# An adaLN transformer block: late K blocks and the Q of chunks 1 to 3 projected between the pairs of the first attention steps

## Chip, cores and metric

One core of one Trainium2 chip runs the kernel. The metric is the device time of one execution in microseconds, the median of the runs. Before the change it is 1879.76 us (three runs, 1879.09 to 1879.83). All times below are microseconds unless marked otherwise.

## What is computed

A transformer block with adaptive layer norm, on x of 2048 rows (S) by 512 (D), 32 heads of 16, and a gated FFN of 1792 columns (F), all in float32:

```python
mod = (silu(c) @ w_mod).reshape(1, 6, 1, 512)
sa, ca, ga, sb, cb, gb = mod[:, 0], ..., mod[:, 5]
h = layernorm(x) * (1 + ca) + sa
q, k, v = split_heads(h @ wqkv)                  # 32 heads, 16 each
p = softmax(q @ k.T * 16 ** -0.5)
x = x + ga * (merge_heads(p @ v) @ wo)
h = layernorm(x) * (1 + cb) + sb
x = x + gb * ((silu(h @ w_gate) * (h @ w_up)) @ w_down)
```

## The kernel before

**Numbers in two parts.** The matmuls run in a rounded format (F32R). To keep accuracy every operand is held as a high part and a low part (the rest), and every product is three matmuls: high x high, high x low, low x high (`mm3`, L205; `accumulate`, L709). "Splitting" a tensor means making these parts: a copy into F32R and a subtraction.

**Projection.** The rows of x go in four chunks of 512. `prep` (L175) normalises a chunk, turns it by transposes and modulates it into `hT[ci]`, high and low. `proj_T(ci, w, m)` (L360) makes one block of 128 columns of Q (w = 0) or K (w = 1) for one chunk: 12 full matmuls into a PSUM bank (four slices of the contraction, three products each), then ACT copies the high part to `prt`, DVE subtracts the low part (L367, L369), and two DMAs on the queue of SyncE (SP) store the three planes to `qd` or `kd` in DRAM (L372, L373). `proj_v` (L388) makes V for 128 rows and leaves it in SBUF as `v_sb`. There are 16 Q blocks, 16 K blocks and 16 V blocks. The class `Stream` (L64) runs a list of such jobs on the PE and, per matmul, lets other generators ("lanes": normalisation `p`, weight splits `w`, modulation vectors `m`) emit one item every so many matmuls.

**Attention.** A unit is one chunk of 512 queries and one group of four heads; 32 units of 16 steps, 512 steps. A step is one block of 128 keys. Its work is four *pairs* and two *P·V halves*. A pair (`pair_of`, L903) is a score matmul (`score`, L500, 50 rows of the array) for the current step and a max matmul (`max_one`, L470, 48 rows) for a step about 20 steps ahead, side by side in the two halves of the array's rows. ACT takes the score's exponential (L508) into one of `PTS` buffers `pt`; DVE reduces the max matmul's bank to row maxima (L481). When a unit's maxima are complete, `max_rows` (L483) turns them and writes them as two more rows of the unit's Q operand, so that the score comes out with its maximum taken off. A P·V half (`pv_step`, L510) is matmuls on four column tiles into bank 7 for half of the queries. Operands are loaded per unit: `load_k` (L462) brings all keys of the head group from `kd` into one of three tiles `kop`, `load_q` (L465) the queries from `qd`.

**PSUM.** Eight banks. Before attention and in plain attention, max matmuls turn through banks 0 to 3 and scores through 4 to 6; bank 7 is P·V's. While FFN work is filled in, it takes banks 3 and 6 (`FBANKS`), max turns through 0 to 2 and scores through 4 and 5.

**Order of the work, written out by hand** (the PE executes in program order, as every engine does):

1. A loop over chunks 0 to 2 (L415) runs the jobs of K, Q and V with the lanes in between.
2. `late` (L836) holds what is left: all of chunk 3, two blocks of chunk 2, and V of chunks 2 and 3: 18 blocks. 48 of their matmuls run at once (L840, L842), the others, 8 or 9 per step, between the max matmuls of 20 lead-in steps (L888 to L897; `LEAD` = 21).
3. The 512 steps. `plain` (L936) does windows of three pairs followed by one or two P·V halves. From step 147 (`STARTS`) each finished chunk's output projection and FFN run half-row matmuls, two side by side on the two halves of the array, between the pairs: `filled` (L949) does eight pairs with places such as `TWO` (0, 3, 2, 2, 2, 2, 1, 0) giving how many of them follow each pair, then P·V.
4. A tail for the last chunk's output projection and FFN.

`close_unit` (L844) does a unit's division by the softmax sum over DRAM and issues the loads for the unit three ahead; `after` (L869) runs what is due at the end of each step. GpSimd (POOL) splits the weights of output projection and FFN once, during the first 128 steps (`split_weights`, L575): it loads raw weights, makes both parts and stores them in `wo_dr`, `gu_dr` and `wd_dr`; the chunks later load both parts. POOL also splits activations during the FFN (L781, L782) and issues half of the operand loads.

Of the kernel before, what the change touches and what calls it, by code (L numbers as in the profile page):

```python
# [43 lines left out]
PTS = 13  # L44
# [4 lines left out]
STARTS = (147, 275, 403)  # L49
TWO = (0, 3, 2, 2, 2, 2, 1, 0)  # L50
# [51 lines left out]
def block_kernel(ctx, tc, x, wqkv, wo, w_gate, w_up, w_down, c, w_mod, out):  # L102
# [33 lines left out]
    gu_dr = dram.tile([NF, P, 4, NK, P], F32, name="gu_dr")  # L136
    wd_dr = dram.tile([NF // FG, P, 2, FG, D], F32, name="wd_dr")
    wo_dr = dram.tile([NK // 2, P, 2, 2, D], F32, name="wo_dr")
# [81 lines left out]

    es_a0 = ExitStack()
# [38 lines left out]
    wqs = [pa0.tile([P, NK, 3 * D], F32R, name=f"wqs{i}") for i in range(2)]  # L260
# [39 lines left out]
    def split_w(src, c0, eng=nc.gpsimd):  # L300
        cols = slice(c0, c0 + P)
        split(wqs[0][:, :, cols], wqs[1][:, :, cols], src, eng)

    def new_hT():
        return [pa0.tile([P, NK, CW], F32R, name=f"hT{i}", tag=f"hT{i}", bufs=2) for i in range(2)]
# [53 lines left out]

    def proj_T(ci, w, m):  # L360
        def job():
            pt = bank("pt")
            col = (0 if w == 0 else D) + m * P

            def post():
                prt = pa0.tile([P, 2, CW], F32R, name="prt", tag="prt", bufs=4)
                nc.scalar.copy(prt[:, 0, :], pt)  # L367
                yield
                nc.vector.tensor_sub(prt[:, 1, :], pt, prt[:, 0, :].bitcast(F32))  # L369
                yield  # L370
                dst = (qd, kd)[w][m * P:(m + 1) * P, :, ci * CW:(ci + 1) * CW]
                nc.sync.dma_start(dst[:, 1 - w:3 - w, :], prt.bitcast(F32))  # L372
                nc.sync.dma_start(dst[:, 2 * w, :], prt[:, 0, :].bitcast(F32))  # L373
            return mm3(pt, lambda a, k: wqs[a][:, k, col:col + P], lambda b, k: hT[ci][b][:, k, :], NK), post()
        return job
# [12 lines left out]
    def proj_v(t):  # L388
        def job():
            pt = bank("pv_")  # L390
            sl = slice((t % 4) * P, (t % 4 + 1) * P)
            h_ = hT[t // 4]

            def post():
                nc.scalar.copy(v_sb[:, t, :, 0:DH], pt.rearrange("p (h d) -> p h d", d=DH))
                yield
            return mm3(pt, lambda a, k: h_[a][:, k, sl], lambda b, k: wqs[b][:, k, 2 * D:3 * D], NK), post()
        return job
# [7 lines left out]
    def load_k0(ci):  # L406
        load_parts(kop[0][:, :, ci * CW:(ci + 1) * CW], kd, 0, ci * CW, (ci + 1) * CW)
# [7 lines left out]
    for ci in range(NC - 1):  # L415
        jobs = [proj_T(ci, w, m) for w, m in kq[:6 if ci == NC - 2 else 8]]
        if ci < NC - 2:
            jobs += [proj_v(4 * ci + t) for t in range(4)]
        hT[ci + 1] = new_hT()
        if ci == 0:  # L420
            jobs[0:2] = [both(*jobs[0:2], 6)]
        if ci == 1:
            sm.add("m", 7, mods(4, 3, lambda e, ev: mod_col(ev, [(modc[:, 2 + e], slice(0, NK), 1.0 - e)])))
        if ci == 2:
            sm.add("m", 6, mods(2, 5, lambda e, ev: mod_row(ev, (ga_bc, gb_bc)[e], (1.0, 0.5)[e])))
        if ci:
            sm.add("p", 5 if ci < NC - 2 else 3, prep(pa, xt[ci + 1], hT[ci + 1], 0, 1))
        for i, _ in enumerate(sm.jobs(jobs)):
            if ci == 0 and i == 5:
                half_prep(1, ev)  # L430
                take(weights_, 2)
                sm.add("w", 5, weights_)
            if ci == 0 and i == 24:
                sm.add("p", 5, prep(pa, xt[1], hT[1], 0, 1))
            if i == 40:
                load_k0(ci)
            if i == 44 and ci + 2 < NC:
                load_x(ci + 2)
        while sm.lanes["p"][1]:
            run(sm.lanes["p"][1].pop(0))  # L440
# [10 lines left out]
    pf = None  # L451
# [10 lines left out]
    def load_k(u):  # L462
        load_parts(kop[u % 3], kd, u % NG, 0, S, nc.gpsimd if u > 2 else nc.sync)

    def load_q(u):  # L465
        ci, g = divmod(u, NG)
        qop[u] = pb.tile([P, 2, CW], F32R, name="qop", tag="qop", bufs=3)
        load_parts(qop[u], qd, g, ci * CW, (ci + 1) * CW, nc.gpsimd if u > 2 else nc.sync)

    def max_one(r):  # L470
# [3 lines left out]
        s, qt, kc = t // 8, t // 2 % 4, t % 2 * 2 + e  # L474
# [35 lines left out]
    def pv_step(i, half):  # L510
# [4 lines left out]
        if kt == 0 and half == 0:  # L515
            pv[u] = single("pv")
            o_[u] = pf.tile([P, CW], F32, name="o", tag="o", bufs=2)
# [10 lines left out]
    def out_a(u, eng):  # L528
        pv.pop(u)
        o = o_.pop(u)  # L530
        dn = pf.tile([P, 16], F32, name="dn", tag="dn", bufs=1)
# [8 lines left out]
    def out_r(u, eng, o):  # L540
        rb = pf.tile([P, CW], F32, name="rb", tag="rb", bufs=1)
# [3 lines left out]
    def out_c(u, eng, mul, o, rb):  # L545
        ci, g = divmod(u, NG)
        on = pf.tile([P, CW], F32, name="on", tag="on", bufs=1)
        mul.tensor_mul(on, o, rb)  # L548
        eng.dma_start(o_dr[ci, g], on)
# [10 lines left out]
    def tile_gu():  # L560
        return pf.tile([P, 4, NK, P], F32R, name="wgu", tag="wgu", bufs=2)

    def tile_wd():
        return pf.tile([P, 2, FG, D], F32R, name="wd", tag="wd", bufs=1)
# [10 lines left out]
    def split_weights():  # L575

        def raw(src, k):
            t = tile_mid().bitcast(F32)
            nc.gpsimd.dma_start(t.rearrange("p e c -> p (e c)").rearrange("p (k c) -> p k c", k=k), src)
            return t  # L580

        def parts(hi, lo, t):
            nc.gpsimd.tensor_copy(hi, t)
            nc.gpsimd.tensor_sub(lo, t, hi.bitcast(F32))

        def store(dst, w):
            nc.gpsimd.dma_start(dst, w.bitcast(F32))

        def cols(m):
            return slice(m * FG * P, (m + 1) * FG * P)  # L590

        srcs = [(wod[:, 2 * k:2 * k + 2, :], 2) for k in range(NK // 2)]
        for m in range(NF // FG):
            srcs += [(wgd[:, :, cols(m)], NK), (wud[:, :, cols(m)], NK), (wdd[:, m * FG:(m + 1) * FG, :], FG)]
        ahead = [raw(*srcs.pop(0)) for _ in range(2)]
        yield

        def following():
            if srcs:
                ahead.append(raw(*srcs.pop(0)))  # L600
            return ahead.pop(0)

        for k in range(NK // 2):
            t = following()
            nc.gpsimd.tensor_mul(t, t, ga_bc[:, None, :].to_broadcast([P, 2, D]))
            w = tile_gu()
            parts(as_wo(w)[:, 0], as_wo(w)[:, 1], t)
            store(wo_dr[k], as_wo(w))
            yield
        for m in range(NF // FG):  # L610
            ws = [tile_gu() for _ in range(FG)]
            for e in range(2):
                t = following()
                src = t.rearrange("p e c -> p (e c)").rearrange("p (k f c) -> p f k c", k=NK, f=FG)
                for f in range(FG):
                    parts(ws[f][:, 2 * e], ws[f][:, 2 * e + 1], src[:, f])
                    if e:
                        store(gu_dr[m * FG + f], ws[f])
# [448 lines left out]
```

## Time and profile before

| | us |
|---|---|
| median of three runs | 1879.76 |
| span of the profiled execution | 1875.6 |
| attention's first score | 189.1 |
| first matmul of the first chunk's output projection (step 147) | 547.9 |
| last max matmul | 1648.8 |

The profile's span is the execution's own time from its first to its last instruction; the runs' times lie some 4 above it. The profile lists for each engine how long it was busy. The engines are PE (TensorE matmuls), PEld (weight loads of the PE, which overlap), DVE (VectorE), ACT (ScalarE), POOL (GpSimd) and SP (SyncE, which here only issues DMAs). A line such as "L481 DVE ... x2048 | 1286.5, 682 | 119.5 <-PE bank L479 72.4" is a group of instructions of one source line: count, busy time in all, mean nanoseconds of one, then the idle time of the engine just before them and what ended most of it. Several matmuls are in flight at once, so the distance between two starts, not the duration of one, tells what a matmul costs.

### The profile page before, as it was taken

The numbers are of one execution on the slowest core, as the hardware profiler recorded it, in microseconds if no ns is written. First come the engines' busy times: TensorE is split into PE (matmuls) and PEld (weight loads), VectorE is DVE, ScalarE is ACT, GpSimd is POOL, SyncE is SP. The second block draws the span as 40 slices with busy tenths as digits, with TensorE's granted clock in tenths as the row PEclk, the third lists the DMA queues.
The fourth block names the chain that finished last, engine by engine and source line by source line (L and its number), as shares of the span: only waits on it lengthen the run. The fifth ranks groups of instructions, "written<-read, shape, count | busy, mean of one in ns | idle before, by whom it ended". The sixth has DMA issues, their size and how long they took to land.

```text
span 1875.6 us, 41002 instructions
## 1 busy us (share of the span) xinstructions
PE 1846.7 (98%) x16996; PEld 1160.4 (62%) x16996; DVE 1541.8 (82%) x2558; ACT 1252.4 (67%) x2406; POOL 415.3 (22%) x498
## 2 busy tenths in 40 slices
PE   7999999999999999999999999999999999999999
PEld 5766444444455766666555667666554566667887
DVE  5548999999999888888999888889999988831643
ACT  4221888888887766777777776677878877674211
POOL 3000454456323211111133111111123011030200
PEclk9999999999999999999999999999999999999999
DMA  8855677766843534554454454453643446243642
GB/s 286 292 198 142 174 183 178 201 167 190 211 86 78 145 102 124 144 124 90 107 124 116 108 127 131 121 122 78 159 86 56 108 92 156 86 159 119 249 180 110
DMA packets 78854, 267.62 MB, mean 143 GB/s; under 512 B 17364, under 2 KB 22484, under 8 KB 57988
## 3 DMA queue, kind: packets, MB, share of 16 engines
q1 hardware_dynamic: 59820, 180.10, 33.0%
q0 software_dynamic: 18160, 84.10, 19.0%
q8 instruction: 133, 2.18, 0.5%
q10 hardware_dynamic: 688, 0.80, 0.1%
q14 instruction: 53, 0.43, 0.1%
HBM read 201.85 MB, written 62.13 MB: 141 GB/s over the span
## 4 chain that ended last, share of the span: by engine, by line
PE 95%; DVE 2%; ACT 2%; DMA 0%; issue 0%; SPq 0%; ACTq 0%; DVEq 0%
PE bank L521 26%; PE bank L506 22%; PE bank L719 19%; PE bank L479 10%; PE bank L729 7%; PE bank L209 7%; DVE mx L481 1%; PE bank L762 1%; PE bank L491 1%; PE bank L162 0%; PE bank L703 0%; DMA wm_ab<-in_w_mod 0%; DVE stt L745 0%; PE bank L279 0%; PE bank L493 0%; PE bank L492 0%
## 5 line engine op out<-in xcount | busy, mean ns | idle before, releaser
L481 DVE TENSOR_REDUCE mx<-bank 128x1 f32<-128x512 f32 x2048 | 1286.5, 682 | 119.5 <-PE bank L479 72.4
L479 PE MATMUL bank<-kop,qop 48*128 48x512 f32 x2048 | 748.0, 432 | 3.6 <-DVE mx L481 3.4
L506 PE MATMUL bank<-qop,kop 50*128 50x512 f32 x2048 | 742.1, 427 | 4.6 <-ACT pt__20499 L508 0.5
L506 PEld LDWEIGHTS bank<-qop,kop 50*128 50x128 f32 x2048 | 347.0, 184 | 305.6 <-issue 63.3
L479 PEld LDWEIGHTS bank<-kop,qop 48*128 48x128 f32 x2048 | 343.9, 184 | 30.7 <-DVE mx L481 14.4
L719 PE MATMUL bank<-act,wgu 64*128 64x512 f32 x1872 | 297.9, 392 | 0.0
L719 PEld LDWEIGHTS bank<-act,wgu 64*128 64x128 f32 x1872 | 188.4, 187 | 30.9 <-DVE m L779 0.3
L548 POOL TENSOR_TENSOR on<-o,rb 128x512 f32<-128x512 f32 x31 | 39.7, 1282 | 442.9 <-DMA rb<-d_dr 304.0
L719 PE MATMUL bank<-wd,mid 64*128 64x512 f32 x912 | 136.5, 397 | 0.0
L781 POOL CAST mid<-m 128x512 fp32r<-128x512 f32 x40 | 24.3, 609 | 430.1 <-PE bank L479 165.5
L719 PEld LDWEIGHTS bank<-wd,mid 64*128 64x128 f32 x912 | 93.3, 185 | 12.0 <-issue 0.8
L209 PE MATMUL bank<-hT,wqs 128*128 128x512 f32 x384 | 95.7, 399 | 2.1 <-DVE prt L369 0.8
L209 PEld LDWEIGHTS bank<-hT,wqs 128*128 128x128 f32 x384 | 70.3, 188 | 24.3 <-issue 6.1
L777 DVE SCALAR_TENSOR_TENSOR q<-th,bank 128x512 f32<-128x512 f32 x56 | 37.7, 673 | 57.4 <-ACT th L773 57.2
L773 ACT ACTIVATE th<-bank 128x512 f32<-128x512 f32 x56 | 33.2, 593 | 58.3 <-PE bank L729 57.9
L793 DVE TENSOR_TENSOR x<-bank,x 128x512 f32<-128x512 f32 x84 | 53.8, 684 | 20.4 <-PE bank L506 20.2
L369 DVE TENSOR_TENSOR prt<-bank,prt 128x512 fp32r<-128x512 f32 x32 | 22.0, 688 | 46.5 <-ACT prt L367 46.5
L367 ACT CAST prt<-bank 128x512 fp32r<-128x512 f32 x32 | 18.8, 587 | 60.2 <-PE bank L209 46.9
L779 DVE TENSOR_TENSOR m<-bank,q 128x512 f32<-128x512 f32 x56 | 38.7, 691 | 21.2 <-PE bank L729 19.1
L729 PE MATMUL bank<-wd,mid 128*128 128x512 f32 x216 | 52.1, 394 | 0.4 <-DVE mid L782 0.3
L782 POOL TENSOR_TENSOR mid<-m,mid 128x512 fp32r<-128x512 f32 x40 | 51.6, 1291 | 3.3
L719 PE MATMUL bank<-wgu,act 64*128 64x512 f32 x288 | 47.7, 394 | 0.1
(6282 smaller groups left out, 5155.0 us busy)
## 6 DMA issues: line engine op xcount, KB each, us to landing
wgu<-gu_dr SPq DMA_DIRECT2D x48, 1024.0 KB
wd<-wd_dr SPq DMA_DIRECT2D x28, 1024.0 KB
kop<-kd SPq DMA_DIRECT2D x33, 768.0 KB
kop<-kd POOLq DMA_DIRECT2D x29, 768.0 KB, 8.5
gu_dr<-wgu POOLq DMA_DIRECT2D x14, 1024.0 KB, 14.1
kd<-prt SPq DMA_DIRECT2D x16, 512.0 KB
qd<-prt SPq DMA_DIRECT2D x16, 512.0 KB
kop<-gu_dr SPq DMA_DIRECT2D x8, 1024.0 KB
```

Of the source, the lines that this page charges most:

```text
L209: nc.tensor.matmul(pt, lhs(a, k), rhs(b, k), start=(n == 0), stop=(n == 3 * nk - 1))
L479: nc.tensor.matmul(pm, qop[u][rows, s, qt * P:(qt + 1) * P], kop[u % 3][rows, s, kc * CW:(kc + 1) * CW], start=True, stop=True)
L481: nc.vector.tensor_reduce(mx[u][:, b, s, qt, kc:kc + 1], pm, op=ALU.max, axis=AX.X)
L506: nc.tensor.matmul(sp, kop[u % 3][rows, h // 2, kt * P:(kt + 1) * P], qop[u][rows, h // 2, :], start=True, stop=True)
L521: nc.tensor.matmul(pv[u][32 * h:32 * h + 32, cols], v_flat[:, e0:e0 + 32], p_[h][:, cols], start=(kt == 0 and half == 0), stop=(kt == 15), ...
L548: mul.tensor_mul(on, o, rb)
L719: nc.tensor.matmul(outs[e], lhs(e, a, k)[rows], rhs(b, k)[rows], start=(ph == 0 and j == 0), stop=(j == z and (ph == 1 or trade is not None)),
L729: nc.tensor.matmul(outs[e], lhs(e, a, k), rhs(b, k), start=(j == 0), stop=(j == z))
L777: nc.vector.scalar_tensor_tensor(q, th, 1.0, outs[0], op0=ALU.add, op1=ALU.mult)
L779: nc.vector.tensor_mul(m32, outs[1], q)
L782: (nc.gpsimd if slow else nc.vector).tensor_sub(mid[:, 1, :], m32, mid[:, 0, :].bitcast(F32))
L793: nc.vector.tensor_add(ch.x2[:, t, :], outs[e], ch.x2[:, t, :])
```

## The change

Projection before attention is cut to chunk 0's Q and K, the first K block (m = 0) of chunks 1 and 2, and V of chunks 0 and 1. `late` becomes the first K block of chunk 3, the second K block of chunks 1 to 3, and V of chunks 2 and 3. The other 18 blocks, K blocks 2 and 3 of chunks 1 to 3 and all of Q of chunks 1 to 3, are made in attention's first 99 steps.

```diff
+HELD = 99
+SOON = (0, 1, 1, 1, 1, 0)
+LATER = (0, 0, 1, 1, 1, 0)
-PTS = 13
+PTS = 14
...
-    for ci in range(NC - 1):
-        jobs = [proj_T(ci, w, m) for w, m in kq[:6 if ci == NC - 2 else 8]]
...
+    first_jobs = [proj_T(0, w, m) for w, m in kq]
+    first_jobs[0:2] = [both(*first_jobs[0:2], 6)]
+    first_jobs += [proj_T(1, 1, 0)] + [proj_v(t) for t in range(4)] + [proj_T(2, 1, 0)] + [proj_v(4 + t) for t in range(4)]
+    for i, _ in enumerate(sm.jobs(first_jobs)):
...
+        if i == 24:
+            hT[1] = new_hT()
+            sm.add("p", 3, prep(pa, xt[1], hT[1], 0, 1))
...
+        if i == 90:
+            hT[2] = new_hT()
+            sm.add("p", 3, prep(pa, xt[2], hT[2], 0, 1))
...
+        if i == 157:
+            hT[3] = new_hT()
+            sm.add("p", 2, prep(pa, xt[3], hT[3], 0, 1))
...
-    late = sm.jobs([proj_T(last, w, m) for w, m in kq[:1] + kq[2:]] + [proj_T(last - 1, w, m) for w, m in kq[6:]] +
-                   [proj_T(last, *kq[1])] + [proj_v(4 * ci + t) for ci in (last - 1, last) for t in range(4)])
+    late = sm.jobs([proj_T(3, 1, 0)] + [proj_T(ci, 1, 1) for ci in range(1, NC)] + [proj_v(t) for t in range(8, NT)])
     ones_rows(1)
     load_q(0)
-    take(late, 22)
-    load_k0(last)
-    take(late, 26)
...
-        take(late, 9 if i % 2 else 8)
+        take(late, 7)
...
+    def late_pair(ci, w, ms):
+        fill = [banks[b] for b in FBANKS]
+        wts = [weight_T(w, m) for m in ms]
+
+        def after():
+            posts_ = [keep_T(ci, w, m, fill[e]) for e, m in enumerate(ms)]
+            for _ in range(3):
+                for p in posts_:
+                    next(p, None)
+        return accumulate(fill, lambda e, a, k: wts[e](a)[:, k, :], lambda b, k: hT[ci][b][:, k, :], NK, after, True)
+
+    def late_pairs():
+        for ci in range(1, NC):
+            yield from late_pair(ci, 1, (2, 3))
+        for ci in range(1, NC):
+            for ms in ((0, 1), (2, 3)):
+                yield from late_pair(ci, 0, ms)
+
+    def mixed(places, work):
+
+        nonlocal four, bank
+        four, bank = three, Turn(4, 5)
+        for k in places:
+            pair_of()
+            take(work, k)
+        pvs(3 if done > 8 else 0, True)
+        end_steps()
...
+    work = late_pairs()
+    while done < 4 * HELD:
+        mixed(SOON if done < 108 else LATER, work)
```

`keep_T` is the tail of the old `proj_T`: the copy, the subtraction and the two stores. In `accumulate` with halves, one `take` emits two matmuls on 64 rows each, one for each of two output blocks; a pair of blocks takes 24 of them. Unit 0's max matmuls are reordered so that all of them for key chunk 0 come first, then chunk 1, and so on, and `load_k0(3)` moves into the fourth lead-in step.

The weights wqkv and all `hT` now have to live until step 99, so memory is found elsewhere: the FFN's tiles (`pf`) are opened only after step 99, the multiplication of a unit's output is done in place, and GpSimd no longer keeps split weights in DRAM. `relay_gu` copies the raw gate and up weights from DRAM to DRAM in the order of use (28 DMAs on POOL's queue, one block every six steps from step 8 on); `relay_weights` scales the output and down weights by their modulation rows from step 102 to 129. The chunks load one raw copy (half the bytes) and split it in place each time:

```diff
+        def halves(self, hi, lo, alone):
+            (nc.scalar.copy if alone else nc.gpsimd.tensor_copy)(hi, lo.bitcast(F32))
+            (nc.vector if alone else nc.gpsimd).tensor_sub(lo, lo.bitcast(F32), hi.bitcast(F32))
+
+        def split_gu(self, f, alone=False):
+            if f < NF and f not in self.split:
+                self.split.add(f)
+                self.halves(self.w[f][:, 0::2], self.w[f][:, 1::2], alone)
...
-            for places in (TWO, TWO) if job is gate_up else (DOWN,):
-                filled(places, work)
+            if job is not gate_up:
+                filled(DOWN, work)
+                continue
+            filled(TWO, work)
+            ch.split_gu(args[0] + 1)
+            filled(TWO, work)
+            if args[0] % FG:
+                ch.split_wd(args[0] // FG)
```

There are now three gate/up tiles (two before) and two down tiles (one before), and gate/up blocks are loaded two ahead. In the tail (`alone`) ACT and DVE do the splitting, three blocks ahead.

240 lines of the change are left out of this document (129 added, 111 removed).

## The prediction

> **What bounds the kernel now.** I read the page's busy table first, then a table of stretches, then the timelines of single stretches. All numbers are microseconds unless marked.
>
> ```profile
> span 1875.6 us, 41002 instructions
> PE 1846.7 (98%) x16996; PEld 1160.4 (62%) x16996; DVE 1541.8 (82%) x2558; ACT 1252.4 (67%) x2406; POOL 415.3 (22%) x498
> ```
>
> A PE that is 98% busy says little by itself, since ends of matmuls are modelled. The stretches say more. The first three rows below are all engines; in the two rows after them the same stretches hold only L209, the projections' matmul line.
>
> ```profile
> 18.80:128.40 109.60, 107.78 (x511) 84.24 (x511) 54.18 (x99) 38.75 (x70) 14.21 (x11) 1.00 0.76 265
> 128.40:189.00 60.60, 58.18 (x255) 38.52 (x254) 52.75 (x87) 8.71 (x16) 0.00 (x0) 1.00 0.55 157
> 225.00:465.00 240.00, 239.88 (x2408) 112.38 (x2408) 238.50 (x407) 209.61 (x414) 123.06 (x128) 1.00 0.70 183
> ```
>
> ```profile
> 18.80:128.40 109.60, 97.93 (x407) 75.26 (x407) 1.00 0.76 265
> 128.40:189.00 60.60, 43.83 (x169) 29.98 (x168) 1.00 0.55 157
> ```
>
> The columns are PE, its weight loads, DVE, ACT, POOL (busy and count), granted clock, DMA share, GB/s. Up to 189 the PE bounds: it projects, 407 and 169 matmuls, with DVE at half and then at 87%. From 189 on, in the plain attention steps (four score/max pairs and two P·V halves each), DVE bounds: 238.5 of 240, nearly all of it the max reduction. The granted clock is 1.00 throughout. How long 99 such steps take now:
>
> ```profile
> L481 DVE TENSOR_REDUCE mx<-bank 128x1 f32<-128x512 f32 x397 | 239.3, 677 | 1.3 <-PE bank L479 0.7 <-PE bank L506 0.3
> L506 PE MATMUL bank<-qop,kop 50*128 50x512 f32 x397 | 137.8, 438 | 0.4 <-ACT v_flat L395 0.2 <-ACT pt__1439 L508 0.2
> ```
>
> These are the groups by line between 189 and 430: 397 scores, 99 steps and one score, in 241, so 2.43 a step. The scores' own matmul line waits for nothing (0.4 in all); the reductions follow each other without a gap.
>
> **The early part: what is removed.** 48 blocks of 12 full matmuls are projected before attention (32 of Q and K, 16 of V). The change leaves 18 in the first loop and 12 in the 20 lead-in steps; 18 blocks, 216 matmuls, go to the attention steps.
>
> ```profile
> 117.00 11.49 PE L209 MATMUL bank<-hT,wqs 128*128 128x512 f32 x48
> 121.88 1.85 SPq L404 DMA_DIRECT2D qop<-qd  x2
> 128.42 0.73 PE L479 MATMUL bank<-kop,qop 48*128 48x512 f32 x4
> ```
>
> 48 of them go from 117.00 to 128.42: 0.238 each, so 216 x 0.238 = 51 off. Of that 192 (46) leave the stretch to 128.4 and 24 (6) the lead-in. Would another engine then bound? In the first stretch DVE's 54.2 loses 16 subtractions and ACT's 38.8 as many copies:
>
> ```profile
> L369 DVE TENSOR_TENSOR prt<-bank,prt 128x512 fp32r<-128x512 f32 x32 | 22.0, 688 | 46.5 <-ACT prt L367 46.5
> L367 ACT CAST prt<-bank 128x512 fp32r<-128x512 f32 x32 | 18.8, 587 | 60.2 <-PE bank L209 46.9 <-DMA kd<-prt 7.4 <-issue 3.9
> ```
>
> That leaves about 43 and 29 in 109.6 - 46 = 64: both fit. In the lead-in the PE has 224 matmuls left (53) against 80 reductions at 0.6 and four subtractions (51): it still bounds. Two covers get thinner. The normalisations of chunks 1 to 3, so far one lane item per five or three matmuls, come per three, three and two; the last has about six of DVE work ahead of its transposes in 22 matmuls (5.2). I take 2 lost (0 to 5). And the 48 matmuls above also covered the load of the first Q operand: issued 4.9 after they began, landed at most 6.5 later since the first max didn't wait. Now the max matmuls follow the first loop at once. Between nothing (the last four blocks there are V, which stores nothing ahead of that load on SP) and 11.4 I take 3, nearer to nothing because SP is free early. **Early part: -51 + 5 = -46**, between -51 and -35.
>
> **The 99 mixed steps: what is added.** They become 66 groups of six pairs, three or four fills (a fill is two half-row matmuls side by side) and three P·V halves. 18 x 4 + 48 x 3 = 216 fills, so all of the 18 blocks. The half-row form over hT and wqs has no row yet; the FFN's fills have the same shape and are the nearest row:
>
> ```profile
> 704.57 0.40 PE L521 MATMUL bank<-pt__7853,v_flat 128*32 128x256 f32 x1
> 705.46 0.38 PE L521 MATMUL bank<-pt__7911,v_flat 128*32 128x256 f32 x1
> 706.43 0.50 PE L506 MATMUL bank<-qop,kop 50*128 50x512 f32 x1
> 706.77 0.39 PE L506 MATMUL bank<-qop,kop 50*128 50x512 f32 x1
> 707.00 0.87 PE L719 MATMUL bank<-act,wgu 64*128 64x512 f32 x6
> 707.71 0.41 PE L506 MATMUL bank<-qop,kop 50*128 50x512 f32 x1
> 710.51 0.40 PE L506 MATMUL bank<-qop,kop 50*128 50x512 f32 x1
> 710.75 0.40 PE L719 MATMUL bank<-act,wgu 64*128 64x512 f32 x2
> 710.99 0.42 PE L506 MATMUL bank<-qop,kop 50*128 50x512 f32 x1
> 711.34 0.40 PE L521 MATMUL bank<-pt__7945,v_flat 128*32 128x256 f32 x1
> ```
>
> A pair or a fill takes a slot of 0.24 (710.51, 710.75, 710.99; three fills 707.00 to 707.71); the first after a switch 0.34 (706.43 to 706.77); P·V begins 0.35 after the last pair (710.99 to 711.34); its four halves last 1.86 up to the next pair (704.57 to 706.43), of which two are 0.89, so a half is 0.43 and three last 1.43. By slots alone a group with three fills is 0.34 + 7 x 0.24 + 0.35 + 1.43 = 3.80, one with four 4.04. DVE needs six reductions, and its pitch is (18.04 - 0.68)/29 = 0.60 by this row, so 3.6:
>
> ```profile
> 188.60 18.04 DVE L481 TENSOR_REDUCE mx<-bank 128x1 f32<-128x512 f32 x30
> ```
>
> Were that all, the fills would be nearly free. But the mixed steps give banks 3 and 6 to the fills, so scores turn through two banks (4 and 5) instead of three, and the pattern puts only 0 or 1 slot between pairs where the FFN's puts 2 or 3. A score then waits until the exponential of the score two before it has read its bank. No row shows that wait on two banks. Its parts do have rows: the exponentials beside the scores above, and the only place where a score does wait, on three banks, at attention's start:
>
> ```profile
> 706.96 0.60 ACT L508 ACTIVATE pt__8001<-bank 128x512 f32<-128x512 f32 x1 [1.53 <-PE bank L479]
> 707.46 0.59 ACT L508 ACTIVATE pt__8006<-bank 128x512 f32<-128x512 f32 x1
> 708.15 0.60 ACT L508 ACTIVATE pt__8017<-bank 128x512 f32<-128x512 f32 x1
> ```
>
> ```profile
> 191.03 0.49 PE L506 MATMUL bank<-qop,kop 50*128 50x512 f32 x1 [0.19 <-ACT pt__1439 L508]
> 191.51 0.49 PE L506 MATMUL bank<-qop,kop 50*128 50x512 f32 x1
> ```
>
> ```profile
> 190.38 0.60 ACT L508 ACTIVATE pt__1439<-bank 128x512 f32<-128x512 f32 x1
> 190.87 0.59 ACT L508 ACTIVATE pt__1444<-bank 128x512 f32<-128x512 f32 x1
> ```
>
> An exponential starts 0.53 after a score that opens a run (706.43, 706.96), 0.44 after one within it (707.71, 708.15), lasts 0.60 and follows another by 0.49. Its bank's next score starts 0.05 after its end (190.98 to 191.03; 191.46 to 191.51), and a score that waited shows 0.49 like one that opens a run. Now a group with three fills, from its first pair at 0:
>
> - pair 0 at 0, exponential 0.53 to 1.13; pair 1 at 0.34, exponential 1.02 to 1.62
> - pair 2 waits for 1.13 + 0.05 = 1.18 (by slots 0.58); exponential 1.71 to 2.31; fill at 1.52
> - pair 3 at 1.76 (its bank is free at 1.67); exponential 2.20 to 2.80; fill at 2.00
> - pair 4 waits for 2.36; exponential 2.89; fill at 2.70; pair 5 at 2.94 (bank free at 2.85)
> - P·V at 3.29, next group at 3.29 + 1.43 = 4.72
>
> With four fills the first of them goes into the gap ahead of pair 2, and the group is as long: the stall, not the fills, sets it. P·V waits for nothing (its steps were scored a group ago; 14 buffers of P hold what stays open), and DVE (3.6) now idles a fifth. At each of the nine late pairs' ends two copies and two subtractions (0.59 and 0.69 each) fall into ACT's and DVE's idle time, and the next fill comes a P·V and two or three pairs later, so I cost them at nothing; with that cover gone they'd be 9 x 2.6 = 23. Their 36 stores go to SP; their readers load six steps or more later. 66 x 4.7 = 310; 6 for the row transposes, about 1 a unit, which now also take a turn of the two banks (an estimate from three slots and a release above); -3 for the first two groups, which have no P·V. **Mixed steps: 313 - 241 = +72.** Bounds: were a waiting score as quick as any other (0.43) and its release 0, the same walk gives 4.43, 19 less; 0.2 more for fills or copies in the way gives 13 more.
>
> On this the Trainium skill has a rule: TensorEngine Tiling (Array Packing), section PSUM Bottleneck, says that tiling makes the matmuls faster and not the emptying of PSUM, which may then bound. As a rate the rows put ACT's emptying at 6 x 0.49 = 2.9 a group, below DVE's 3.6, so by rate alone the sum would be that of the slots; it is the latency over two banks that the walk above charges for.
>
> **FFN stretches and the tail: what moves.** GpSimd no longer splits weights once during the first 128 steps; it splits each weight tile again for every chunk, while the FFN runs.
>
> ```profile
> L583 POOL CAST wd<-mid 128x1024 fp32r<-128x1024 f32 x5 | 5.2, 1039 | 0.3
> L584 POOL TENSOR_TENSOR wd<-mid,wd 128x1024 fp32r<-128x1024 f32 x5 | 11.9, 2380 | 0.4
> ```
>
> ```profile
> 640.00:880.00 240.00, 240.00 (x2524) 164.71 (x2522) 210.06 (x331) 168.81 (x325) 33.99 (x40) 1.00 0.50 122
> ```
>
> ```profile
> L782 POOL TENSOR_TENSOR mid<-m,mid 128x512 fp32r<-128x512 f32 x14 | 18.1, 1290 | 1.2
> L548 POOL TENSOR_TENSOR on<-o,rb 128x512 f32<-128x512 f32 x5 | 6.4, 1290 | 57.2 <-DMA rb<-d_dr 53.7 <-ACT pt__8947 L508 3.5
> ```
>
> A split costs 1.04 + 2.38 = 3.4. Three per two gate/up pairs and two down pairs (six groups, six times 711.34 - 704.57 = 6.8, so 41) are 10 where POOL is busy 34 of 240 now: cover enough. Each split is queued half a gate/up pair (6.8) or more before its use; what stands ahead of it in POOL's queue is the split of the activations (1.9) and, once a unit, the multiplication that waits for a DMA (57.2/5 = 11). Loads halve, and the new DRAM-to-DRAM copies run while POOL is nearly free. In the tail ACT and DVE split instead, in a stretch where the PE bounds. I take +2, between -3 (smaller loads) and +12.
>
> **Sum.** -46 + 72 + 2 = +28 on the profiled span of 1875.6, so 1904; the median of the runs, 1879.76, lies 4.2 above that span, so **1908**.
>
> **Rivals.**
> (B) The two banks don't hold the scores up: a group takes its slots, 18 x 4.04 + 48 x 3.80 = 255, with the same extras 258, +17. Sum -46 + 17 + 2 = -27: **1853**. For it: the FFN's groups run on two banks with no visible stall. Against: their pairs are 0.7 apart except the last. It decides below (241 + 46 - 2 - 3)/66 = 4.27 a group.
> (C) POOL splits late: 11 of DMA wait plus 3.4 against 6.8 of lead leave 7.6 once a unit, and some 13 units close during FFN stretches: up to 99 more, **1908 to 2007**. Against: POOL is 86% idle there and that multiplication is queued at about the time its data come.
> (D) The early part doesn't shrink as counted, at its bound -35: **1919**.
>
> **How the numbers follow.** The walk of the group 0.76; B 0.12; C 0.05; D 0.07, inside the walk's spread. The walk's own range: 1908 - 19 - 3 = 1886 below, and above 1908 + 13 + 11 = 1932, which leaves out B, most of C and little else: **1886 to 1932**. About 0.2% can be told from no change here (4). Faster 0.13 (B and a little), same 0.03, slower 0.84.
>
> **What would show it.** After: attention's first pair near 143; the first FFN fill of step 147 some 26 later than now; in the mixed stretch groups 4.7 apart, scores waiting for an exponential twice a group, and DVE near 78% busy there. Groups at 3.8 would make me wrong by sign; waits of FFN matmuls for POOL's splits, or a first pair later than 155, by size.

## The result and the profile after

| | before | after |
|---|---|---|
| median of the runs, taken side by side | 1879.6 | 1940.12 (1938.09 to 1941.79) |
| span of the profiled execution | 1875.6 | 1937.4 |
| first max matmul | 128.4 | 93.6 |
| attention's first score | 189.1 | 163.1 |
| first FFN matmul of step 147 | 547.9 | 601.0 |
| last score | 1711.3 | 1764.9 |

The changed kernel is slower, by a ratio of 1.032 (95% interval 1.0308 to 1.0335). The forecast was 1908 with a range of 1886 to 1932: the sign was right, the loss more than twice as large as forecast (61.8 between the spans, against 28).

Differences of the rows above give the stretches. Up to the first max it is 34.8 shorter; the lead-in, from there to the first score, is 69.5 instead of 60.7; from the first score to step 147 it takes 437.9 instead of 358.8 (+79.1); the FFN stretches last 1163.9 instead of 1163.4; from the last score to the end it is 172.5 instead of 164.3 (+8.2). The two rows that head the page of the changed kernel, and its table of stretches (engines, granted clock, DMA share, GB/s):

```profile
span 1937.4 us, 41575 instructions
PE 1865.5 (96%) x17212; PEld 1158.9 (60%) x17212; DVE 1572.2 (81%) x2579; ACT 1281.4 (66%) x2427; POOL 575.8 (30%) x566
```

```profile
18.80:93.60 74.80, 67.07 (x319) 48.30 (x317) 44.97 (x83) 27.64 (x51) 17.22 (x15) 0.95 0.75 264
93.60:163.10 69.50, 59.23 (x233) 36.37 (x232) 51.61 (x85) 9.01 (x16) 0.00 (x0) 0.90 0.33 80
205.00:480.00 275.00, 250.55 (x2432) 124.35 (x2424) 218.74 (x364) 196.85 (x370) 34.02 (x46) 1.00 0.47 114
1764.90:1937.40 172.50, 163.86 (x724) 129.91 (x720) 93.45 (x138) 46.69 (x66) 17.00 (x17) 0.99 0.26 89
```

Before, the first two of these stretches had a granted clock of 1.00 and a PE busy for all but 2 of 110 and 2 of 61. Now the PE idles for 10 in the lead-in, at a clock of 0.90. In the mixed steps DVE is busy 218.74 of 275, 80%, so it no longer sets the pace there.

**The early part: a store behind bulk loads.** The tile `prt`, into which `keep_T` copies a block before it is stored, has two buffers (L376, `bufs=2`); the old `proj_T` had four (L366). A copy must therefore wait until the stores of the block two before it are done. ACT's timeline of the changed kernel, three of those copies, with the idle time ahead and what ended it in brackets:

```profile
45.73 0.59 ACT L377 CAST prt<-bank 128x512 fp32r<-128x512 f32 x1 [5.41 <-DMA qd<-prt]
55.61 0.58 ACT L377 CAST prt<-bank 128x512 fp32r<-128x512 f32 x1 [5.92 <-DMA qd<-prt]
125.32 0.58 ACT L377 CAST prt<-bank 128x512 fp32r<-128x512 f32 x1 [16.27 <-DMA kd<-prt]
```

What was issued ahead of the store on SP's queue in the lead-in:

```profile
106.80 1.74 SPq L423 DMA_DIRECT2D kop<-kd  x4
108.58 1.06 SPq L423 DMA_DIRECT2D qop<-qd  x2
109.69 1.46 SPq L382 DMA_DIRECT2D kd<-prt  x1
112.20 0.65 SPq L382 DMA_DIRECT2D kd<-prt  x1
```

Unit 1's K and Q loads (L423) go out from 106.80 on and the stores of two blocks follow at 109.69 and 112.20; the copy that needs the first of these buffers starts at 125.32. In the first loop the two waits above are for stores issued at 37.30 and 47.07 on the same queue, soon after a load of rows of x (32.55) and loads of w_mod (41.10). In the lead-in ACT stands still, behind it DVE's subtraction and the max reductions, and with the reductions the PE. The PE's timeline:

```profile
58.60 1.11 PE L302 MATMUL bank<-ident,ev 128*128 128x128 f32 x4 [4.47 <-ACT ev L296]
...
116.29 1.88 PE L212 MATMUL bank<-ws,hT 128*128 128x512 f32 x7
127.29 2.59 PE L504 MATMUL bank<-kop,qop 48*128 48x512 f32 x4 [9.12 <-DVE mx L506]
129.80 3.35 PE L212 MATMUL bank<-ws,hT 128*128 128x512 f32 x7
```

The idle time of 9.12 is not all. The seven projection matmuls after it take 3.35, those before it 1.88. The stretches around it, whose third value from the end is the granted clock:

```profile
118.00:127.30 9.30, 0.18 (x2) 0.01 (x1) 1.36 (x3) 1.07 (x2) 0.00 (x0) 0.69 0.87 239
127.30:131.00 3.70, 3.70 (x7) 2.13 (x8) 3.70 (x7) 0.00 (x0) 0.00 (x0) 0.50 0.58 215
131.00:137.00 6.00, 6.00 (x21) 3.52 (x19) 2.90 (x5) 0.59 (x1) 0.00 (x0) 0.65 0.01 3
137.00:163.10 26.10, 25.01 (x109) 15.80 (x107) 22.52 (x37) 3.51 (x7) 0.00 (x0) 1.00 0.00 1
```

After the idle time the clock is 0.50, then 0.65 on average, and from 137 on 1.00. The Trainium skill, page "TensorE: Matmul & The Clock Gate", Part 1, section "What's actually happening", describes this: half rate after at least one idle window of some 3.4, full rate again after at least one busy window of that length. These rows agree in the half rate (0.50). The way back was long here: if the clock has only these two values, 0.65 over 6.0 puts another 4.2 at half rate, so that full rate returns some 7.9 after work sets in at 127.3 (an estimate from the second and third row), more than two such windows.

**The mixed steps.** The PE's timeline of one group with four fills. Shown are the scores (L531), with the wait in brackets, and the first P·V matmul (L546); the max matmuls and fills between them are left out:

```profile
205.89 0.50 PE L531 MATMUL bank<-qop,kop 50*128 50x512 f32 x1
206.23 0.39 PE L531 MATMUL bank<-qop,kop 50*128 50x512 f32 x1
...
207.08 0.50 PE L531 MATMUL bank<-qop,kop 50*128 50x512 f32 x1 [0.22 <-ACT pt__1596 L533]
207.65 0.42 PE L531 MATMUL bank<-qop,kop 50*128 50x512 f32 x1
208.26 0.49 PE L531 MATMUL bank<-qop,kop 50*128 50x512 f32 x1
208.82 0.42 PE L531 MATMUL bank<-qop,kop 50*128 50x512 f32 x1
209.19 0.40 PE L546 MATMUL bank<-pt__1537,v_flat 128*32 128x256 f32 x1
...
210.62 0.49 PE L531 MATMUL bank<-qop,kop 50*128 50x512 f32 x1
```

From the group's start the pairs stand at 0, 0.34, 1.19, 1.76, 2.37 and 2.93, P·V at 3.30, the next group at 4.73. The walk of the prediction had 0, 0.34, 1.18, 1.76, 2.36, 2.94, 3.29 and 4.72. The mixed steps end at 482.70.

**FFN and tail.** From the groups by line of the FFN stretches, the loads of the gate/up matmuls as weights, with their waits; then the tail of the kernel before in its table of stretches, beside the last row of the table above; then the last block of the tail's down product in the PE's timeline:

```profile
L738 PEld LDWEIGHTS bank<-act,wgu 64*128 64x128 f32 x1872 | 188.4, 187 | 29.8 <-POOL wgu L657 0.2 <-issue 0.2
```

```profile
1711.30:1875.60 164.30, 159.82 (x724) 128.82 (x720) 69.64 (x117) 27.36 (x45) 10.95 (x14) 0.99 0.46 176
```

```profile
1924.69 0.50 PE L748 MATMUL bank<-wd,mid 128*128 128x512 f32 x1 [2.38 <-ACT wd L656]
1925.95 7.19 PE L748 MATMUL bank<-wd,mid 128*128 128x512 f32 x23 [0.76 <-DVE wd L657]
```

GpSimd's split of a weight tile was waited for 0.2 in all over the 1872 weight loads. In the tail the last down weights come late: 2.38 for ACT's copy, 0.76 for DVE's subtraction, one matmul in between.

### The profile page after: what moved, and what is told of

The parts are those of the page before. It is cut to its first block, busy times and chain, and to the rows that moved or that the text cites. A ratio compares the mean times of both kernels' runs of the same rounds, so it can differ in the third digit from the quotient of the medians.

```text
span 1937.4 us, 41575 instructions
## 1 busy us (share of the span) xinstructions
PE 1865.5 (96%) x17212; PEld 1158.9 (60%) x17212; DVE 1572.2 (81%) x2579; ACT 1281.4 (66%) x2427; POOL 575.8 (30%) x566
## 4 chain that ended last, share of the span: by engine, by line
PE 89%; ACT 4%; DMA 3%; DVE 3%; issue 0%; SPq 0%; ACTq 0%; DVEq 0%
PE bank L546 25%; PE bank L531 22%; PE bank L738 21%; PE bank L504 9%; PE bank L748 6%; PE bank L212 3%; DVE mx L506 1%; DMA qd<-prt 1%; DMA kd<-prt 1%; PE bank L516 1%; DVE stt L764 1%; PE bank L722 0%; PE bank L518 0%; PE bank L517 0%; DMA wm_ab<-in_w_mod 0%
## 5 line engine op out<-in xcount | busy, mean ns | idle before, releaser
L531 PE MATMUL bank<-qop,kop 50*128 50x512 f32 x2048 | 774.1, 430 | 29.9 <-ACT pt__2870 L533 0.6
L504 PE MATMUL bank<-kop,qop 48*128 48x512 f32 x2048 | 780.1, 435 | 11.3 <-DVE mx L506 11.0
L531 PEld LDWEIGHTS bank<-qop,kop 50*128 50x128 f32 x2048 | 350.0, 184 | 362.4 <-issue 81.8
L572 POOL TENSOR_TENSOR rb<-o,rb 128x512 f32<-128x512 f32 x31 | 39.9, 1286 | 450.7 <-DMA rb<-d_dr 312.7
L657 POOL TENSOR_TENSOR wgu<-wgu 128x1024 fp32r<-128x1024 f32 x48 | 114.5, 2385 | 4.0
L423 POOL DMA_DIRECT2D kop<-kd x29 | 17.0, 585 | 329.7 <-PE bank L738 189.5
L738 PE MATMUL bank<-hT,wl 64*128 64x512 f32 x432 | 88.9, 395 | 0.0
L212 PE MATMUL bank<-ws,hT 128*128 128x512 f32 x192 | 54.5, 426 | 0.0
L657 POOL TENSOR_TENSOR wd<-wd 128x1024 fp32r<-128x1024 f32 x21 | 50.2, 2390 | 1.7
L656 POOL CAST wgu<-wgu 128x1024 fp32r<-128x1024 f32 x48 | 50.3, 1047 | 0.0
```

Of the source, the lines that this page charges most:

```text
L212: nc.tensor.matmul(pt, lhs(a, k), rhs(b, k), start=(n == 0), stop=(n == 3 * nk - 1))
L504: nc.tensor.matmul(pm, qop[u][rows, s, qt * P:(qt + 1) * P], kop[u % 3][rows, s, kc * CW:(kc + 1) * CW], start=True, stop=True)
L531: nc.tensor.matmul(sp, kop[u % 3][rows, h // 2, kt * P:(kt + 1) * P], qop[u][rows, h // 2, :], start=True, stop=True)
L572: mul.tensor_mul(rb, o, rb)
L656: (nc.scalar.copy if alone else nc.gpsimd.tensor_copy)(hi, lo.bitcast(F32))
L657: (nc.vector if alone else nc.gpsimd).tensor_sub(lo, lo.bitcast(F32), hi.bitcast(F32))
```

## The experiments

The theory after this reading: three separate costs. (1) Two buffers of `prt` behind the bulk loads, with the clock that falls after the stall: some 20. (2) Two score banks with only 0 or 1 fill between pairs; the fills themselves cost less. (3) The tail's late split: some 5. The rivals: the fills as such are the cost, or the losses are shadows of something else and come back elsewhere when one is mended. All edits are made to the changed kernel unless another is named. e1 to e7 are single executions. Those of them whose code is the changed kernel's up to the first score reach it at 160.4 to 162.8, the changed kernel at 163.1, so a difference of 3 in one stretch may be chance.

**e1: no fills, two score banks.** Of the late blocks' matmuls only one pair for each block pair is left, with the copies and stores.

```diff
-        return accumulate(fill, ..., NK, after, True)
+        def one():
+            for e in range(2):
+                rows = slice(64 * e, 64 * e + 64)
+                nc.tensor.matmul(fill[e], wts[e](0)[rows, 0, :], hT[ci][0][rows, 0, :], start=True, stop=True)
+            after()
+            yield
+        return one()
...
-        mixed(SOON if done < 108 else LATER, work)
+        mixed((0, 0, int(done // 6 % 7 == 2), 0, 0, 0), work)
```

> Of each late block's twelve products only one is made, over half of the contraction; 9 fills are left of 216, scores still turn through banks 4 and 5. Theory (a score's wait for the exponential two before it sets the group): groups stay at 4.7 us and the time within 5 us of the changed kernel's 1940. Rival (the fills' own slots set the group): 207 fills of 0.24 go, the time falls by up to 50, to about 1890.

Measured: 2005.13, with less work slower by 65. Both theories missed. Two stretches of it, and three pairs from a short stretch at full clock:

```profile
200.00:300.00 100.00, 87.35 (x628) 36.33 (x630) 68.53 (x113) 60.47 (x114) 10.09 (x14) 0.78 0.40 95
700.00:1700.00 1000.00, 995.48 (x10254) 631.09 (x10247) 899.37 (x1458) 742.62 (x1427) 364.07 (x347) 1.00 0.42 87
```

```profile
214.86 0.50 PE L531 MATMUL bank<-qop,kop 50*128 50x512 f32 x1
215.20 0.39 PE L531 MATMUL bank<-qop,kop 50*128 50x512 f32 x1
216.04 0.49 PE L531 MATMUL bank<-qop,kop 50*128 50x512 f32 x1 [0.45 <-ACT pt__1526 L533]
```

The third pair still starts 1.18 after the first, as walked, and its wait is now 0.45 instead of 0.22: the fill that stood in the gap is gone, the gap is not. But the granted clock fell to 0.78 in 200 to 300, where the changed kernel, with the fills, had 1.00. So the run can't price the stall by itself.

**e2: no fills, three score banks.** As e1 (the same part left out), and `mixed` turns through the banks of plain attention:

```diff
-        four, bank = three, Turn(4, 5)
+        four, bank = Turn(0, 1, 2, 3), Turn(4, 5, 6)
```

> As the run before, with the same products left out, but scores turn through banks 4 to 6 and max matmuls through 0 to 3. Theory: pairs at 0, 0.34, 0.58, 1.18, 1.67 and 2.16, P.V at 2.51, next group at about 3.95: 66 x 0.78 = 51 less than with two banks, about 1889. Rival (the bunching of six pairs ahead of P.V, not the banks, makes the group long): 4.7 a group, 1940.

Measured: 1921.77; the first score to step 147 takes 417.2, that is 20.7 less than with fills on two banks. A group in the PE's timeline:

```profile
210.34 0.49 PE L531 MATMUL bank<-qop,kop 50*128 50x512 f32 x1
...
211.53 0.50 PE L531 MATMUL bank<-qop,kop 50*128 50x512 f32 x1 [0.21 <-ACT pt__1580 L533]
...
214.37 0.49 PE L531 MATMUL bank<-qop,kop 50*128 50x512 f32 x1
```

Now the fourth pair waits instead of the third, 1.19 after the first, and a group takes 4.03 instead of 4.73, near the 3.95 of the theory: a third score bank shortens the group (the maxima have a fourth bank here too, but the pair waits for an exponential). That would be 46 over 66 groups, and only 20.7 came. Most of the rest is lost where a block pair's one remaining fill stands, at nine places: it takes banks 3 and 6, through which maxima and scores now turn too. There the fills wait 8.1 in all for an exponential and the maxima 5.4 for the block's subtraction. The granted clock, 0.91 in 163 to 200, 0.97 in 200 to 300 and 0.95 in 300 to 400, accounts for some 11 more (an estimate: 37 x 0.09 + 100 x 0.03 + 100 x 0.05). So this run doesn't give the price of the two banks either.

**e3: the same fills in groups of eight pairs.** The fills stay half-row matmuls in banks 3 and 6, and in the groups that carry them the scores stay on two banks; the pattern is that of the FFN's groups, two or three fills between most pairs. 18 groups with 12 fills each make the 216; the other 63 of the 99 steps are plain, on three score banks.

```diff
-    while done < 4 * HELD:
-        mixed(SOON if done < 108 else LATER, work)
+    for _ in range(18):
+        filled(TWO, work)
+    plain(HELD - done // 4)
```

> The same 216 fills, all work done, in 18 groups of eight pairs with the FFN's places (0, 3, 2, 2, 2, 2, 1, 0) and four P.V halves, then 63 plain steps up to step 99; still two score banks. Theory: 18 x 6.8 + 63 x 2.44 = 276 in place of some 316, so about 1900, with no score waiting. Rival (the price is that of the fills' slots): no change, 1935 to 1940.

Measured: 1900.08, as expected; the first score to step 147 takes 401.6 instead of 437.9. A group in its PE timeline; then the scores up to step 147 as a group by line (163 to 601), first of the changed kernel, then of e3:

```profile
209.14 0.50 PE L531 MATMUL bank<-qop,kop 50*128 50x512 f32 x1
...
209.71 0.86 PE L738 MATMUL bank<-hT,wl 64*128 64x512 f32 x6
...
215.90 0.50 PE L531 MATMUL bank<-qop,kop 50*128 50x512 f32 x1
```

```profile
L531 PE MATMUL bank<-qop,kop 50*128 50x512 f32 x590 | 236.3, 448 | 25.8 <-ACT pt__2870 L533 0.6 <-ACT pt__3447 L533 0.6 <-ACT pt__4541 L533 0.6
L531 PE MATMUL bank<-qop,kop 50*128 50x512 f32 x633 | 227.6, 430 | 2.7 <-ACT pt__5488 L533 1.0 <-ACT pt__2693 L533 0.6 <-ACT pt__1980 L533 0.5
```

With equal work the pattern is worth 36 of the 79: in the dense groups the scores hardly wait on two banks, and the plain steps have their third bank back. The waits of the scores account for 23 of the 36 (25.8 - 2.7); the other 13 were not taken apart. What is left of the 79 is 42.8 (401.6 - 358.8). The 18 groups last 126.0 (161.1 to 287.07) where 36 plain steps of 2.43 take 87.5, so 38.5 of it, or 0.178 for each of 216 fills, against the 0.238 that a full matmul cost before attention; the other 4.3 lie in the plain steps behind them.

**e4: unit 1's loads six lead-in steps later.** Nothing else is changed.

```diff
             load_k0(3)
+        if i == -LEAD + 9:
             load_k(1)
             load_q(1)
```

> Only the loads of unit 1's K and Q are issued six lead-in steps later. Theory (with two buffers for the projected block the copy waits for a store that is queued behind these loads): the 9 us without a matmul at 118 go, and the low clock after it; the first score comes at 147 to 151 instead of 163 and the time falls by 12 to 16, to 1924 to 1928. Rival (the lead-in is long for another reason, such as the order of unit 0's maxima or the load of K chunk 3): the stall stays, 1938 to 1941.

Measured: 1930.13, 10.0 less where 12 to 16 were expected, with the first score at 151.7. The lead-in, at full clock again, in the table of stretches:

```profile
95.30:151.70 56.40, 55.64 (x231) 34.49 (x230) 51.56 (x85) 9.10 (x16) 0.00 (x0) 1.00 0.40 98
```

56.4 instead of 69.5: the loads on SP's queue were the cause of the long wait. The 13.1 are the 9.1 of idle time and 4.0 of slow clock after it (3.7 at 0.50 and 6.0 at 0.65 lose that much). Whether the store waits its turn in the queue or is slowed by the load on the DMA engines (share 0.87 in 118 to 127.3) isn't separated by this. The stalls of the first loop are still there (first max at 95.3).

**e5: three buffers for the blocks.** The memory for the third comes from the scratch that the kernel sets aside for DMA descriptors.

```diff
-        prt = pr.tile([P, 2, CW], F32R, name="prt", tag="prt", bufs=2)
+        prt = pr.tile([P, 2, CW], F32R, name="prt", tag="prt", bufs=3)
...
-    nc = _bacc.Bacc("TRN2", ..., dynamic_dma_scratch_size=4096)
+    nc = _bacc.Bacc("TRN2", ..., dynamic_dma_scratch_size=2048)
```

> A third buffer for the projected block (the memory comes from halving the space set aside for DMA descriptors); nothing else. Theory (a copy waits for the store two blocks back, which is queued behind bulk loads): in the lead-in the fourth block's copy now waits for a store issued seven us earlier, so the 9 us stall at 118 and the half clock after it go, and the stall at 52 to 57 shrinks; the first score comes at 145 to 150 instead of 163, the time falls by 13 to 18, to 1922 to 1927. Rival (the DMA engines' load itself, which a buffer doesn't change): 1936 to 1941.

Measured: 1923.03. First loop and lead-in in the table of stretches:

```profile
18.80:87.10 68.30, 62.97 (x312) 46.68 (x310) 45.45 (x83) 28.06 (x51) 16.34 (x14) 1.00 0.79 283
87.10:143.50 56.40, 55.61 (x231) 34.49 (x230) 51.52 (x85) 9.11 (x16) 0.00 (x0) 1.00 0.39 98
```

Both stalls go and the clock is 1.00. The first score comes at 143.5, 19.6 earlier. Of these, 16.2 reach the end; the other 3.4 go in the later stretches, each a little longer than in the changed kernel (438.8 to step 147, 1165.8 for the FFN stretches, 173.1 for the tail).

**e6: late blocks one by one with full matmuls.** One bank (3) for the fills, so that bank 6 goes back to the scores; 216 full matmuls in place of 216 pairs of half-row ones.

```diff
+    def late_block(ci, w, m):
+        fill, wt = banks[3], weight_T(w, m)
+        for i, _ in enumerate(mm3(fill, lambda a, k: wt(a)[:, k, :], lambda b, k: hT[ci][b][:, k, :], NK)):
+            if i == 3 * NK - 1:
+                run(keep_T(ci, w, m, fill))
+            yield
...
-        four, bank = three, Turn(4, 5)
+        four, bank = three, Turn(4, 5, 6)
```

> The same 66 groups, places and number of fills, all work done, but a fill is one full matmul into bank 3 alone, and scores turn through banks 4, 5 and 6. Theory: pairs at 0, 0.34, 0.58, then bounded by the three max banks 1.26, 1.87, 2.47, next group at 4.3 instead of 4.73; 66 x 0.43 = 28 less, about 1911. Rival (the third score bank is worth nothing, the bunching of the pairs is all): 4.7, about 1940.

Measured: 1962.03, slower than the changed kernel: another miss. The PE's timeline around one fill (L212), then the starts of two groups:

```profile
206.19 0.39 PE L531 MATMUL bank<-qop,kop 50*128 50x512 f32 x1
206.51 0.50 PE L212 MATMUL bank<-hT,wl 128*128 128x512 f32 x1
206.94 0.49 PE L531 MATMUL bank<-qop,kop 50*128 50x512 f32 x1
...
212.12 0.50 PE L531 MATMUL bank<-qop,kop 50*128 50x512 f32 x1
...
217.66 0.49 PE L531 MATMUL bank<-qop,kop 50*128 50x512 f32 x1
```

No score waits here. But from pair to full matmul it takes 0.32 and from there to the next pair 0.43: 0.75 where two half-row slots take 0.48. The pair after that, again with one full matmul between, follows 0.85 later (206.94 to 207.79). A group is 5.54 long. The Trainium skill, page "TensorEngine Tiling (Array Packing)", section "Key Properties", says that a change of the tiling mode drains the TensorE; these rows agree, at 0.27 to 0.37 for a change there and back. The third score bank is paid for with that much at every fill.

**e7: the tail's last down weights split earlier.** In the tail they are split after the second to last down product's block instead of with the last gate/up block.

```diff
-                if f % FG:
+                if f % FG and f < NF - 1:
                     ch.split_wd(f // FG, True)
+            elif ch.ci == last and args == (NF // FG - 2, 2):
+                ch.split_wd(NF // FG - 1, True)
```

> In the tail the last pair of down blocks' weights are split by ACT and DVE one gate/up block earlier, ahead of it instead of behind. Theory (the last down product waits 3.1 us for that split, with a low clock after it): the span from the last score to the end falls from 172.5 to 167 or 168, the time by 4 to 5, to 1935. Rival (the tail is longer because ACT and DVE are busier throughout): no change beyond 1.

Measured: 1932.84, 7.3 less than the changed kernel. The last block of the down product in the PE's timeline:

```profile
1920.50 6.34 PE L748 MATMUL bank<-wd,mid 128*128 128x512 f32 x24
```

All 24 in one run, no wait; last score to end 167.8, 4.7 less, as expected. The kernels with the late split (the changed one and e1 to e6) take 171.3 to 178.9 here, those with the early one (e7 to e9) 167.8 to 168.6. Another 2.4 lie before the first score (160.7), where the code is unchanged, and are no effect of the edit. The 3.5 that remain against 164.3 were not taken apart.

**e8: e4 to e7 together, with full matmuls** in 36 groups with places (0, 1, 2, 1, 2, 0).

> All work done, four edits together: third block buffer, K and Q loads of unit 1 six lead-in steps later, the last split earlier, and the late blocks as full matmuls into one bank in 36 six-pair groups with places (0, 1, 2, 1, 2, 0) and three score banks, then plain steps up to step 99. Theory: first score near 146 (43 ahead of the kernel before); 36 groups of 4.4 in place of 54 steps of 2.43 cost 28, with some 5 for the units' ends; tail +3: 43 - 33 - 3 = 7 below the kernel before, about 1873. Rival (a fill costs in attention what it cost before it, 0.24 each): 216 x 0.24 = 52 on attention, about 1892.

Measured: 1925.78, ratio to the kernel before 1.024 (1.0223 to 1.0252). Both expectations missed. The first score comes at 145.4, so the early repairs hold, but it takes 446.7 from there to step 147, 45 more than e3's half-row fills in dense groups. Two starts of groups in its PE timeline, 6.00 apart:

```profile
205.07 0.50 PE L531 MATMUL bank<-qop,kop 50*128 50x512 f32 x1
...
211.07 0.49 PE L531 MATMUL bank<-qop,kop 50*128 50x512 f32 x1
```

With 4 changes there and back in each of 36 groups, at the 0.27 to 0.37 of e6, the changes cost 39 to 53 (an estimate), as much as the repairs gain before the first score (43.7).

**e9: e3, e5 and e7 together**, the three repairs that had each held by itself, with no other edit.

> The changed kernel with the mixed groups of late K in eight pairs (54 tiles of three halves in 18 groups each carrying four instead of three tiles, the remaining groups plain, as in e3), a third block buffer (as in e5) and the last down weights split earlier (as in e7); whole computation kept. Theory (the three costs of the change are separate and add): first maximum at 87, first score at 143.5 as in e5; first score to step 147 some 401.6 as in e3, so step 147 at about 545; FFN stretch as in the other runs, last score at about 1708; tail 167.8 as in e7; span about 1876 and time about 1879, level with the kernel before (within 5 of it). Rival (they overlap: part of what e3 or e5 saved was the same recovered clock): 1888 or more, with attention longer than 405 or the first score later than 150. What remains of the change's own gain is by the theory nearly nothing: early part and lead-in 46 shorter, attention 43 longer, tail 3.5 longer.

Measured: 1877.57 (1874.86 to 1879.48) beside 1879.17 for the kernel before on the same chip, ratio 0.999 (0.9981 to 0.9999). The head of its page, and the first score and the first FFN matmuls of step 147 in the PE's timeline:

```profile
span 1876.0 us, 41574 instructions
```

```profile
146.38 0.49 PE L531 MATMUL bank<-qop,kop 50*128 50x512 f32 x1
...
543.59 0.96 PE L738 MATMUL bank<-wgu,act 64*128 64x512 f32 x6
```

First max at 89.9 (expected 87), first score at 146.4 (expected 143.5), 397.2 from there to step 147 (expected 401.6), last score at 1707.4, end 168.6 later. The span came out as expected (1876), to the microsecond by luck: 2.9 more before the first score and 4.4 less behind it nearly cancel. Within such differences the costs are separate and add up; the rival (1888 or more, attention longer than 405 or a first score later than 150) falls. Against the kernel before, 42.7 come off before the first score, 38.4 come back between it and step 147 and 4.3 in the tail. So the repaired change is level with the kernel before: 0.1% below it, with an interval that ends just under 1.

## Why the prediction was right or wrong

| step | predicted | measured | apart |
|---|---|---|---|
| first max matmul at | 87.7 | 93.6 | +5.9 |
| lead-in | 55.0 | 69.5 | +14.5 |
| first score to step 147, more than before | +72 | +79.1 | +7.1 |
| FFN stretches and tail, more than before | +2 | +8.7 | +6.7 |

The first two rows are the prediction's -46 in its parts: 192 matmuls by 0.238 off 128.4 and 5 back for the thinner covers, 24 matmuls off the lead-in's 60.7. The four differences make 34, which are the 61.8 - 28 but for a rounding.

**The early part: wrong, and beyond its own bound.** The stretch to the first score became 26 shorter; the prediction said 46, between 35 and 51. The failed step is the question "Would another engine then bound?". It was answered by the busy time of ACT and DVE, and what came was a wait: a buffer of `prt` is released by a DMA, and that DMA is done late when bulk loads were issued ahead of it on SP's queue. The row was on view: before the change that copy already waited 7.4 for a store with four buffers. The change halves them, and the prediction doesn't mention it. Its own sign of a wrong size, a first pair later than 155, came (163.1). e4 and e5 show the cause from two sides: without the loads ahead, or with one buffer more, the lead-in is 56.4 and, in e5, the first max comes at 87.1. Both lie within 1.4 of the predicted 55.0 and 87.7, so the count of the matmuls was right. The 5 charged for thinner covers fit in sum (87.1 is 4.4 above 128.4 - 45.7), but e8 and e9, with the same first loop, reach the first max at 89.0 and 89.9, and no run takes the covers apart. The clock was 1.00 throughout before, and the prediction took it as given; the stall cost 9.1, the slow clock behind it 4.0 more.

**The mixed groups: right in the mechanism.** Pairs, P·V and next group stand within 0.01 of the walk; rival B (slots alone, at most 4.04 a group) is out. The +7.1 lie within the walk's bound of 13. The 66 groups took 319.6 (163.1 to 482.70) instead of 313; the surplus is in the first two groups (8.52 together), the groups in which units end (most 5.82), and those after a block pair's end (4.87 to 4.89 instead of 4.72 in the seven that stand alone, so the copies that were costed at nothing cost about 0.16 a time). The sign of the whole came from here, and e3 confirms the reason: with fills enough between the pairs the waits of the scores drop from 25.8 to 2.7, and 36 come back in all.

**FFN stretches: right.** +0.5; GpSimd's splits are never late, so rival C is out. **Tail: mis-sized.** It was part of +2 within -3 to +12 and cost 8.2, of which 4.7 is the last down weights' split by e7 and 3.5 stays open. The prediction asked whether the PE bounds the tail as a whole, not which split is last in line. **Rival D** (the early part doesn't shrink as counted) was the right kind, but was given -35 at worst, where -26 was measured. **The range** took in the walk's 13 and the early part's 11 above the forecast, but not the 10 that the prediction allowed for FFN and tail; with them it would have reached 1942 and held the result by luck, since the early part lay 9 outside its own bound.

## What to carry to other kernels

Where a buffer is released by a DMA, the number of buffers and what stands ahead of that DMA on its queue belong in the sum, and a busy share says nothing of them. Price a long PE stall with the slow clock that followed it here (4.0 after 9.1). Work moved between other matmuls costs its slots only if the pattern leaves the banks time to be emptied: walk one group by its latencies, then choose the pattern, as e3 did at no cost in memory. Moving 216 matmuls to a stretch where each costs 0.178 (38.4 / 216, e9) instead of 0.238 gains 13 by these numbers, and the small costs of the move use that up: in e9 8.7 of the 51.4 counted don't come off before the first score, and the tail costs 4.3.

## What the runs showed of the hardware

- The clock also falls without one long stall. In e1 the PE was busy 87% in 200 to 300, with no gap longer than 1.0, and the granted clock was 0.78; in the changed kernel's mixed steps, busy 91% of 205 to 480, it was 1.00. The Trainium skill, page "TensorE: Matmul & The Clock Gate", Part 1, section "A second HAM failure mode: psum-queue depth-cycling", tells of such a case, with frequent short idling between groups of matmuls, and e1 agrees. The busy share alone doesn't decide it: in e2, busy 92% of 200 to 300, it was 0.97. Where the border lies was not measured.
- A single full matmul between half-row pairs costs 0.75 to 0.85 from pair to pair, against 0.48 for two half-row slots (e6).
